# Decode step with sliding-window attention and a squared-ReLU MLP: the first wo projection computed ahead of the last K unit's transposes

## The chip, the core and the metric

The kernel runs on one core of one Trainium2 chip. The metric is the device time of one execution in microseconds (us). The core has a matrix engine (PE, with its weight loads listed apart as PEld), a vector engine (DVE), a scalar engine (ACT), GpSimd (POOL) and a sync engine (SP) that here does nothing but start DMA transfers, one after the other in program order. Engines wait for each other through semaphores; an instruction that waits holds up all that stand behind it on its own engine.

## The reference

One token for each of two batch rows is normalised; attention over the last 2048 positions of a cache, and an MLP, are computed from it and added to the input:

```python
B, Sq, D = x.shape                      # 2, 1, 576
Hq, Dh = 32, 128;  Hkv = 16             # two query heads per K/V head
W = min(4096, max(256, Sk // 4))        # 2048 of 8192
q = (x @ wq) split into heads
scores = q . k[:, :, Sk - W:] * Dh ** -0.5
o = softmax(scores) . v[:, :, Sk - W:]
A = o.reshape(B, Sq, Hq * Dh) @ wo      # wo: 4096 x 576
h = relu(x @ w1 + b1) ** 2              # F = 4608
Bm = h @ w2 + b2
return x + A(layernorm(x)) + Bm(layernorm(x))
```

Everything is bf16. K and V windows (16.8 MB each), wq, wo (4.7 MB each), w1 and w2 (5.3 MB each) are read once, 53.6 MB in all; the output is 2 x 576.

## The kernel before

**Units.** The work on the caches is cut into NU = 8 units. A unit u is four K/V heads of one batch row: a K tile and a V tile of 128 partitions x 8192 bf16 (2048 KB each). For each unit PE transposes K in eight groups of four (`transposes(u, g)`, tile kT_ps in PSUM), ACT and DVE copy the groups in turn into kT in SBUF, PE computes the scores (`scores`, sc_ps), DVE/POOL/ACT do the softmax (`softmax_max`, `softmax_exp`, `softmax_tr`, which leaves pT), PE multiplies by V (`pv`, pv_ps), DVE picks the wanted parts (`pv_mix`, tiles mix and acc) and PE sums them per head (`pv_out`, sm). `step(u, p, o)` is the pipeline: transposes and scores of unit u, softmax of u-1, the V product of p, the head sums of o.

**The wo projection.** wo is used in two halves of 2048 rows. When four units are done, `pv_out` lets DVE normalise them and write ws_t (t = 0 after unit 3, t = 1 after unit 7); `wo_acc(t)` is then 32 matmuls of 2 x 288 (16 rows of wo per partition, two column halves each), each with its own weight load of ws_t. They are accumulated into out_ps, the one PSUM tile that also collects the residual, b2 and most of the MLP's second product. The order of the sums within out_ps is free.

**The MLP.** w1 is used early (between units 1 and 2). The second product reads w2 in four parts: w2_0, w2_1, w2_2 (18 matmuls of 2 x 288 each into out_ps, `mlp_o`), and w2_3, loaded in two pieces of 7 and 2 rows (`mlp_tail`, into tail_ps). out_ps is copied to SBUF (part, line 555) and added into tail_ps by eight small matmuls; then tail_ps is copied out and stored.

**Buffers.** K, V and the first three w2 tiles take turns in one pool of six buffers (`kvpool`); w2_3 takes the buffer that held w1. The pool for wo, `wopool`, has **one** buffer: the transfer of the second half, wo_1, has to wait until the first half's last matmul has read wo_0.

**Order.** Each engine runs its instructions in a fixed order. PE's, and most of DVE's and ACT's, follow the program text (`keep_in_program_order`). SP's list of transfers is arranged when the program is built; it follows the text but for small shifts. All large loads go through SP and one DMA queue.

**The end of the program.** The lines that the change and the prediction's steps touch are the last 35 of the kernel: the transfers of the second wo half (line 534, issued at line 118) and of w2 (lines 535 and 536, issued at line 131), `step(NU - 1, NU - 3, NU - 4)`, that is, the transposes of unit 7 with the V product of unit 5 and the head sums of unit 4 (line 537), the V product of unit 6 (539, 540), `wo_acc(0)` (546), the V product of unit 7 (548) and, behind it, the first w2 part, `wo_acc(1)`, and the other w2 parts (550 to 560). Matmuls other than transposes are recorded at line 84, transposes at line 87, loads of K and V at line 106.

Of the kernel before, what the change touches and what calls it, by code (L numbers as in the profile page):

```python
# [16 lines left out]
def kernel(  # L17
# [105 lines left out]
    def issue_w2(g, r0, r1):  # L123
        if g < NG4 - 1:
            tl = kvpool.tile([P, FR * D], BF16, tag="kv", name=f"w2_{g}")[:]
        else:
            if r0 == 0:
                w2_last.append(wbig.tile([P, FR * D], BF16, tag="wbig", name=f"w2_{g}"))
            tl = w2_last[0][:, r0 * D:r1 * D]
        rows = B_w2[g * HW:(g + 1) * HW, :].rearrange("(p r) n -> p (r n)", r=FR)  # L130
        nc.sync.dma_start(out=tl, in_=rows[:, r0 * D:r1 * D])  # L131
        w2_tiles[(g, r0)] = tl
# [99 lines left out]
    def out_acc(lhsT, rhs_of, start=False, stop=False):  # L232
        for i in range(2):
            pe_mm(out_ps[32 * i:32 * i + B, :], lhsT=lhsT, rhs=rhs_of(i * OH, (i + 1) * OH),
                  start=start, stop=stop, skip_group_check=True)
# [36 lines left out]
    def transposes(u, g):  # L272
        k_sb = k_tiles[u]
        w, gw = divmod(g, GW)
        if gw == 0:
            kT_tiles[(u, w)] = ktpool.tile([P, NT, P, 2], BF16, tag="kT_sb", name=f"kT_{u}_{w}")
        kT = kT_tiles[(u, w)]
        kT_ps = psum.tile([P, PG, P], F32, tag="kT", bufs=3, name=f"kT_ps_{u}_{g}")
        for i in range(PG):
            q = g * PG + i  # L280
            pe_tr(out=kT_ps[:, i, :], in_=k_sb[:, 2 * q * Dh:2 * (q + 1) * Dh].bitcast(F32),
                                identity=ident_f[:])
        src = kT_ps[:].rearrange("p i s -> p (i s)").bitcast(BF16)
        dst = kT[:, gw * PG:(gw + 1) * PG, :, :].rearrange("p i s e -> p (i s e)")
        if g % 2 == 0:
            pin(nc.scalar.copy(out=dst, in_=src))  # L286
        else:
            pin(nc.vector.tensor_copy(out=dst, in_=src))  # L288

    def scores(u, w):  # L290
        tq, b = divmod(u, B)
        if w == 0:
            sc_tiles[u] = psum.tile([P, NT, 32], F32, tag="sc", bufs=2, name=f"sc_ps_{u}")
            pe_mm(sc_tiles[u][:].rearrange("p t s -> p (t s)"), lhsT=qhead[:], rhs=khead[:],
                             start=True, stop=False, skip_group_check=True)
        sc_ps = sc_tiles[u]
        kT = kT_tiles.pop((u, w))[:].rearrange("p t s e -> p e t s")
        for e in range(2):
            for k in range(4):
                pe_mm(sc_ps[32 * k:32 * (k + 1), :, :],  # L300
                                      lhsT=qz[:, e, b * NQ + tq, w, :, :].rearrange("p j c -> p (j c)"),
                                      rhs=kT[:, e, :, 32 * k:32 * (k + 1)], start=False, stop=(w == 1 and e == 1),
                                      skip_group_check=True, tile_position=(0, 32 * k))
# [3 lines left out]
    def softmax_max(u):  # L307
        sc_ps = sc_tiles.pop(u)[:].rearrange("p t s -> p (t s)")
        mx = work.tile([P, 1], F32, tag="mx", name=f"mx_{u}")
        pin(nc.vector.tensor_reduce(out=mx[:], in_=sc_ps, axis=AX.X, op=ALU.max))  # L310
        m2 = work.tile([P, NC], F32, tag="m2", name=f"m2_{u}")
        pin(nc.vector.tensor_scalar(out=m2[:], in0=offm[:], scalar1=mx[:, 0:1], scalar2=None, op0=ALU.add))  # L312
        gmax = work.tile([P, NC], F32, tag="gmax", name=f"gmax_{u}")
        nc.gpsimd.partition_all_reduce(gmax[:], m2[:], channels=P, reduce_op=ReduceOp.max)  # L314
        sm_cur[u] = (sc_ps, gmax)

    def softmax_exp(u):
        sc_ps, gmax = sm_cur.pop(u)
        gs = work.tile([P, NC], F32, tag="gs", name=f"gs_{u}")
        pin(nc.vector.tensor_tensor(out=gs[:], in0=gmax[:], in1=own_s[:], op=ALU.mult))  # L320
        nb = work.tile([P, 1], F32, tag="nb", name=f"nb_{u}")
        pin(nc.vector.tensor_reduce(out=nb[:], in_=gs[:], axis=AX.X, op=ALU.add))  # L322
        pr = work.tile([P, NT * 32], BF16, tag="pr", name=f"pr_{u}")
        acc = keep.tile([P, Dh + 1], F32, tag="acc", bufs=4, name=f"acc_{u}")
        pin(nc.scalar.activation(out=pr[:], in_=sc_ps, func=ACT.Exp, bias=nb[:], scale=scale, accum_out=acc[:, Dh:Dh + 1]))  # L325
        sm_cur[u] = (pr, acc)

    def softmax_tr(u):
        pr, acc = sm_cur.pop(u)
        pT = keep.tile([P, NT, 32], BF16, tag="pT", name=f"pT_{u}")  # L330
        pin(nc.vector.transpose(out=pT[:].rearrange("p t m -> p (t m)"), in_=pr[:]))  # L331
        pT_tiles[u], acc_tiles[u] = pT, acc
# [3 lines left out]
    def pv_start(u):  # L336
        pv_cur[u] = psum.tile([P, 4, Dh], F32, tag="misc", name=f"pv_ps_{u}")

    def pv(u, i):
        pv_ps = pv_cur[u]  # L340
        v = v_tiles[u][:].rearrange("p (w t x) -> p t w x", w=2, t=NT)
        for k in range(4):
            t = 4 * i + k
            pe_mm(pv_ps[32 * k:32 * (k + 1), :, :].rearrange("m (w a) d -> m w (a d)", w=2),
                                  lhsT=pT_tiles[u][:, t, :], rhs=v[:, t, :, :], start=(i == 0),
                                  stop=(i == NT // 4 - 1), skip_group_check=True, tile_position=(0, 32 * k))
# [21 lines left out]
    def pv_out(u):  # L368
        tq, b = divmod(u, B)
        t, half = divmod(tq, 2)  # L370
        if u % (2 * B) == 0:
            sm_tiles[t] = psum.tile([P, B, Dh + 1], F32, tag="sm", name=f"sm_{t}")
        sm = sm_tiles[t]
        pe_mm(sm[half * (P // 2):(half + 1) * (P // 2), b, :],
                         lhsT=tohead[:].rearrange("p c x -> p (c x)"), rhs=acc_tiles.pop(u)[:], start=True, stop=True,
                         skip_group_check=True, tile_position=(0, half * (P // 2)))
        if u % (2 * B) == 2 * B - 1:
            ri = work.tile([P, B], F32, tag="ri", name=f"ri_{t}")
            pin(nc.vector.reciprocal(out=ri[:], in_=sm[:, :, Dh]))
            od = work.tile([P, B, DW, WR], F32, tag="od", bufs=1, name=f"od_{t}")  # L380
            for k in range(B):
                nc.vector.scalar_tensor_tensor(out=od[:, k, :, :],
                                               in0=sm[:, k, 0:Dh].rearrange("p (x r) -> p x r", x=DW),
                                               scalar=ri[:, k:k + 1],
                                               in1=own[:].unsqueeze(2).to_broadcast([P, DW, WR]),
                                               op0=ALU.mult, op1=ALU.mult)
            ws = work.tile([P, WR, B], BF16, tag="ws", name=f"ws_{t}")
            with nc.allow_low_precision(reason="sums of one value and zeros"):
                nc.vector.tensor_reduce(out=ws[:], in_=od[:].rearrange("p b x r -> p r b x"), axis=AX.X, op=ALU.add)
            wo_state[t] = ws  # L390

    def wo_acc(tq):
        ws = wo_state.pop(tq)
        wo_sb = wo_tiles.pop(tq)
        for r in range(WR):
            out_acc(ws[:, r, :], lambda a, z: wo_sb[:, r, a:z])
# [86 lines left out]
    def step(u, p=None, o=None):  # L483
        if p is not None:
            pv_start(p)
        transposes(u, 0)
        softmax_max(u - 1)
        transposes(u, 1)
        softmax_exp(u - 1)
        transposes(u, 2)  # L490
        if p is not None:
            pv(p, 0)
        transposes(u, 3)
        if p is not None:
            pv(p, 1)
        softmax_tr(u - 1)
        if o is not None:
            pv_out(o)
        transposes(u, 4)
        scores(u, 0)  # L500
        for g in range(GW + 1, NG):
            transposes(u, g)
        for i in range(2, NR):
            if p is not None:
                pv(p, i)
        if p is not None:
            pv_mix(p)
        scores(u, 1)
# [25 lines left out]
    issue_wo(1)  # L534
    for w in W2P:
        issue_w2(*w)
    step(NU - 1, NU - 3, NU - 4)
    pv_start(NU - 2)
    for i in range(NR):
# [3 lines left out]
    softmax_exp(NU - 1)  # L543
    pv_mix(NU - 2)
    softmax_tr(NU - 1)
    wo_acc(0)
    pv_out(NU - 2)
    pv_all(NU - 1)
    pv_out(NU - 1)
# [48 lines left out]
```

## Time and profile before

| what | value |
|---|---|
| time, median of 3 runs (lowest to highest) | 139.25 us (138.78 to 139.61) |
| time of the profiled execution | 139.34 us |
| its span, first to last instruction | 137.6 us |
| mean granted PE clock | 0.876 |
| busy: PE, PEld | 88.7 us (64%), 54.9 us (40%) |
| busy: DVE, ACT, POOL | 59.6 us (43%), 43.9 us (32%), 7.7 us (6%) |
| read from HBM | 53.62 MB, 390 GB/s over the span |
| SP's DMA queue, share of 16 DMA engines | 92.2% |

How to read the profile: the page cuts the span into 40 equal slices of 3.44 us and gives for each how busy an engine was and what the DMA engines moved. The chain is followed back from the last instruction to whatever released each step. A timeline row gives start, duration, engine, line, operation, output tile and inputs, and in brackets how long the engine had been idle before and what ended the idle time. A windows row gives for a stretch of time its length, the busy time of PE, PEld, DVE, ACT and POOL (with the number of instructions), then the granted PE clock as a share of full speed, the busy share of the DMA engines and the rate in GB/s. "SPq" is the time that SP takes to issue a transfer, not the transfer.

### The profile page before, as it was taken

What the parts mean: (1) busy time and instruction counts of PE and PEld (TensorE: products, weight loads), DVE (VectorE), ACT (ScalarE), POOL (GpSimd) and SP (SyncE); (2) the same over time, 40 slices, a digit from 0 to 9 for tenths busy, and PEclk for the clock granted to TensorE, in tenths of its full rate; (3) what the DMA queues carried; (4) which work ended last, traced back from release to release, by engine and by line L of the source; (5) the groups of instructions that cost most, each with busy time, mean ns of one, the idle gap of its engine ahead of it and who ended that gap; (6) DMA issues with size and microseconds to landing.
All of it is one profiled execution on the core that took longest, in us unless ns stands there. A gap on an engine that the chain in (4) does not pass through costs nothing.

```text
span 137.6 us, 2040 instructions
## 1 busy us (share of the span) xinstructions
PE 88.7 (64%) x830; PEld 54.9 (40%) x830; DVE 59.6 (43%) x151; ACT 43.9 (32%) x63; POOL 7.7 (6%) x26
## 2 busy tenths in 40 slices
PE   0079047979967486696595797991059969408451
PEld 0078012919623454453451743650055524204230
DVE  6935202025551085458449247786005376700021
ACT  2627101014710467282272273670025402000001
POOL 7600000001000010100100100101000010000000
PEclk9999965555899999999999599999555999995999
DMA  4999979999989999999999999999999974799940
GB/s 153 408 514 397 493 326 448 419 426 543 422 346 424 410 453 419 424 453 405 434 453 400 443 441 410 444 426 420 443 434 419 427 302 80 316 401 431 426 194 1
DMA packets 3632, 53.74 MB, mean 391 GB/s; under 512 B 412, under 2 KB 420, under 8 KB 680
## 3 DMA queue, kind: packets, MB, share of 16 engines
q1 hardware_dynamic: 3604, 53.61, 92.2%
q8 instruction: 6, 0.10, 0.3%
q10 hardware_dynamic: 20, 0.01, 0.0%
q14 instruction: 2, 0.02, 0.0%
HBM read 53.62 MB, written 0.00 MB: 390 GB/s over the span
## 4 chain that ended last, share of the span: by engine, by line
DMA 66%; PE 24%; DVE 4%; ACT 2%; SPq 1%; issue 1%; DVEq 0%; ACTq 0%
DMA k<-in_A_k_cache_dram 41%; DMA wq_sb<-in_A_wq_dram 13%; DMA w<-in_B_w_dram 12%; PE kT_ps L87 10%; PE sc_ps L84 3%; PE q_ps L84 3%; PE qs_ps L84 3%; PE pv_ps L84 2%; DVE kT L288 2%; PE out_ps L84 2%; PE sm L84 1%; PE tail_ps L84 1%; ACT kT L286 1%; SPq L131 1%; ACT pr L325 1%
## 5 line engine op out<-in xcount | busy, mean ns | idle before, releaser
L87 PE MATMUL kT_ps<-ident_f,k 128*128 128x128 f32 x256 | 40.6, 314 | 14.4 <-DMA k<-in_A_k_cache_dram 14.0
L286 ACT COPY kT<-kT_ps 128x1024 bf16<-128x1024 bf16 x32 | 32.0, 1010 | 37.3 <-PE kT_ps L87 36.9
L87 PEld LDWEIGHTS kT_ps<-ident_f,k 128*128 128x128 f32 x256 | 33.5, 162 | 23.8 <-issue 20.2
L288 DVE COPY kT<-kT_ps 128x1024 bf16<-128x1024 bf16 x32 | 22.1, 691 | 32.7 <-PE kT_ps L87 32.6
L84 PE MATMUL sc_ps<-kT,qz 128*32 128x512 bf16 x128 | 10.6, 414 | 4.3 <-DVE kT L288 2.8
L84 PE MATMUL pv_ps<-v,pT 128*32 128x512 bf16 x128 | 10.8, 404 | 0.8 <-DVE acc L360 0.8
L314 POOL PARTITION_ALL_REDUCE gmax<-m x8 | 2.9, 365 | 103.9 <-DVE m L312 103.9
L84 PE MATMUL out_ps<-wo,ws 128*2 128x288 bf16 x64 | 5.7, 348 | 4.1 <-DMA wo<-in_A_wo_dram 4.1
L325 ACT ACTIVATE pr<-sc_ps,nb 128x512 bf16<-128x512 f32 x8 | 5.5, 687 | 8.4 <-DVE nb L322 8.4
L84 PE MATMUL q_ps<-wq_sb,xnT 128*4 128x512 bf16 x36 | 4.0, 628 | 5.2 <-DMA wq_sb<-in_A_wq_dram 5.2
L566 ACT CAST fin_sb<-tail_ps 2x144 bf16<-2x144 f32 x2 | 0.5, 272 | 20.3 <-PE tail_ps L84 20.2
L310 DVE TENSOR_REDUCE mx<-sc_ps 128x1 f32<-128x512 f32 x8 | 5.5, 684 | 3.1 <-PE sc_ps L84 3.1
L84 PEld LDWEIGHTS <-xnT 128*4 128x4 bf16 x90 | 2.6, 98 | 10.2 <-issue 9.3
L84 PEld LDWEIGHTS <-qz 128*32 128x32 bf16 x128 | 2.3, 98 | 9.9 <-DVE kT L288 6.2
L555 DVE COPY part<-out_ps 2x288 f32<-2x288 f32 x2 | 0.9, 448 | 12.0 <-PE out_ps L84 12.0
L360 DVE SCALAR_TENSOR_TENSOR mix<-pv_ps,own_j,mix 128x128 f32<-128x128 f32 x16 | 5.6, 351 | 0.6
L84 PEld LDWEIGHTS <-ws 128*2 128x2 bf16 x64 | 3.2, 100 | 6.4 <-issue 3.8
L331 DVE STREAM_TRANSPOSE pT<-pr 128x512 bf16<-128x512 bf16 x8 | 5.6, 702 | 0.2 <-ACT pr L325 0.2
L87 PE MATMUL pro_ps<-ident,xs 2*128 2x2 bf16 x10 | 0.6, 164 | 7.6 <-DVE xs L182 7.6
L84 PE MATMUL out_ps<-w,hT_sb 128*2 128x288 bf16 x54 | 3.8, 285 | 2.2 <-DMA w<-in_B_w_dram 2.2
L84 PEld LDWEIGHTS <-pT 128*32 128x32 bf16 x128 | 2.7, 95 | 5.4 <-issue 3.0
L84 PEld LDWEIGHTS <-hT_sb 128*2 128x2 bf16 x90 | 2.8, 83 | 5.2 <-issue 2.8
(77 smaller groups left out, 61.6 us busy)
## 6 DMA issues: line engine op xcount, KB each, us to landing
k<-in_A_k_cache_dram SPq DMA_DIRECT2D x8, 2048.0 KB, 7.4
v<-in_A_v_cache_dram SPq DMA_DIRECT2D x8, 2048.0 KB, 18.0
w_sb<-in_B_w_dram SPq DMA_DIRECT2D x1, 5184.0 KB, 19.1
wq_sb<-in_A_wq_dram SPq DMA_DIRECT2D x1, 4608.0 KB
wo<-in_A_wo_dram SPq DMA_DIRECT2D x2, 2304.0 KB, 8.7
w<-in_B_w_dram SPq DMA_DIRECT2D x3, 1296.0 KB
w<-in_B_w_dram SPq DMA_DIRECT2D x1, 1008.0 KB
w<-in_B_w_dram SPq DMA_DIRECT2D x1, 288.0 KB
```

Source lines behind the costliest of these rows:

```text
L84: return tc.keep_in_program_order(nc.tensor.matmul(out, **kw))
L87: return tc.keep_in_program_order(nc.tensor.transpose(**kw))
L131: nc.sync.dma_start(out=tl, in_=rows[:, r0 * D:r1 * D])
L286: pin(nc.scalar.copy(out=dst, in_=src))
L288: pin(nc.vector.tensor_copy(out=dst, in_=src))
L310: pin(nc.vector.tensor_reduce(out=mx[:], in_=sc_ps, axis=AX.X, op=ALU.max))
L314: nc.gpsimd.partition_all_reduce(gmax[:], m2[:], channels=P, reduce_op=ReduceOp.max)
L325: pin(nc.scalar.activation(out=pr[:], in_=sc_ps, func=ACT.Exp, bias=nb[:], scale=scale, accum_out=acc[:, Dh:Dh + 1]))
L331: pin(nc.vector.transpose(out=pT[:].rearrange("p t m -> p (t m)"), in_=pr[:]))
L360: op = nc.vector.scalar_tensor_tensor(out=nx, in0=pv_ps[:, j, :], scalar=own_j[:, j:j + 1], in1=acc, op0=ALU.mult, op1=ALU.add)
L555: nc.vector.tensor_copy(out=part[:, i * OH:(i + 1) * OH], in_=out_ps[32 * i:32 * i + B, :])
L566: cp(out=fin_sb[:, q * OQ:(q + 1) * OQ], in_=mlp["out"][32 * k:32 * k + B, :])
```

## The change

One call moves. `wo_acc(0)` stood between the softmax transposition of unit 7 and the head sums of unit 6; it now stands ahead of the last `step`.

```diff
     issue_wo(1)
     for w in W2P:
         issue_w2(*w)
+    wo_acc(0)
     step(NU - 1, NU - 3, NU - 4)
     pv_start(NU - 2)
     for i in range(NR):
...
     softmax_exp(NU - 1)
     pv_mix(NU - 2)
     softmax_tr(NU - 1)
-    wo_acc(0)
     pv_out(NU - 2)
     pv_all(NU - 1)
     pv_out(NU - 1)
```

On PE, before, the scores of unit 6 (sc_ps_999) are followed at once by the transposes of unit 7 (k_821 is its K tile, pT_982 the softmax of unit 5):

```order
 L84 MATMUL sc_ps_999<-kT_1_992,qz 32x512
-L87 MATMUL kT_ps_0_1063<-ident_f,k_821 128x128 x4
-L87 MATMUL kT_ps_1_1075<-ident_f,k_821 128x128 x4
-L87 MATMUL kT_ps_2_1088<-ident_f,k_821 128x128 x4
-L84 LDWEIGHTS pT_982
```

In the changed program the 32 weight loads and 32 matmuls of the first wo half (wo_819 is wo_0, ws_990 is ws_0) stand in between; the last of them and what follows:

```order
+L84 LDWEIGHTS ws_990
+L84 MATMUL out_ps<-wo_819,ws_990 2x288
+L87 MATMUL kT_ps_0_1095<-ident_f,k_821 128x128 x4
+L87 MATMUL kT_ps_1_1107<-ident_f,k_821 128x128 x4
+L87 MATMUL kT_ps_2_1120<-ident_f,k_821 128x128 x4
```

So 64 PE instructions go from behind the softmax of unit 7 to ahead of its transposes; nothing else on PE changes place.

On SP the end of the list of transfers changes as well. Names: v_931 and v_933 are the V tiles of units 6 and 7, wo_1050 is wo_1, w_0 to w_3 the parts of w2; in brackets stand the semaphores that a transfer waits for before it is issued (DMAHW: an earlier transfer has landed; PE: PE has come far enough):

```order
 L106 DMA v_931<-in_A_v_cache_dram 128x1x8192 [waits DMAHW0_49,PE_49]
 L106 DMA v_933<-in_A_v_cache_dram 128x1x8192 [waits DMAHW7_49,PE_49]
-L131 DMA w_0_1052<-in_B_w_dram 128x5184 [waits DMAHW2_49,PE_49]
-L118 DMA wo_1050<-in_A_wo_dram 128x9216 [waits DMAHW4_49,DMAHW1_49,PE_49]
+L118 DMA wo_1050<-in_A_wo_dram 128x9216 [waits DMAHW4_49,PE_49]
+L131 DMA w_0_1052<-in_B_w_dram 128x5184 [waits DMAHW2_49,DMAHW1_49]
 L131 DMA w_1_1054<-in_B_w_dram 128x5184
-L131 DMA w_2_1056<-in_B_w_dram 128x5184 [waits DMAHW5_49,DMAHW3_49]
+L131 DMA w_2_1056<-in_B_w_dram 128x5184 [waits DMAHW5_49,DMAHW3_49,PE_49]
 L131 DMA w_3_1058<-in_B_w_dram 128x4032
 L131 DMA w_3_1058<-in_B_w_dram 128x1152
```

wo_1 changes places with w2_0 and is now the first transfer behind the last V tile, and w2_2 has a wait for PE of its own. The instructions of DVE, ACT and POOL keep their order.

## The prediction

> **What bounds the kernel now.** I read the page first: its span, the rate of the DMA engines slice by slice, and the shares of the chain that ended last.
>
> ```profile
> span 137.6 us, 2040 instructions
> GB/s 153 408 514 397 493 326 448 419 426 543 422 346 424 410 453 419 424 453 405 434 453 400 443 441 410 444 426 420 443 434 419 427 302 80 316 401 431 426 194 1
> DMA 66%; PE 24%; DVE 4%; ACT 2%; SPq 1%; issue 1%; DVEq 0%; ACTq 0%
> ```
>
> The transfers run at 400 to 450 GB/s nearly everywhere, and two thirds of the chain is DMA: this is a stream of bytes with arithmetic beside it. The exception is late: slices 32 to 34 of the 40 (110 to 120 us) show 302, 80 and 316 GB/s. Next the chain in order of time, from the landing of the last K tile on, says what the stream waited for there.
>
> ```profile
> 74.18 26.99 DMA k<-in_A_k_cache_dram
> ...
> 113.38 2.07 PE out_ps L84 x32
> 115.47 0.33 SPq L118
> ...
> 116.81 16.70 DMA w<-in_B_w_dram
> 133.55 1.29 PE tail_ps L84 x44
> ```
>
> PE's 32 matmuls of the first wo half end at 115.45, SP issues wo_1 at 115.47, the last large transfer lands at 133.51 (116.81 + 16.70), PE's last 44 matmuls end at 134.84. SP's own waits after 86 us, and its timeline, give the reason.
>
> ```profile
> SPq L118 <- PE out_ps L84: 19.1, 1, 19.1
> SPq L131 <- PE kT_ps L87: 6.2, 1, 6.2
> SPq L118 <- DMA wo<-in_A_wo_dram: 3.9, 1, 3.9
> ```
> ```profile
> 83.89 1.18 SPq L106 DMA_DIRECT2D v<-in_A_v_cache_dram  x2
> 92.14 0.33 SPq L131 DMA_DIRECT2D w<-in_B_w_dram  x1
> 115.86 2.19 SPq L131 DMA_DIRECT2D w<-in_B_w_dram  x4
> ```
>
> SP issued V of units 6 and 7 at 84 and w2_0 at 92.14, and then stood at wo_1 from 92.47 to 115.47: 3.9 us for the landing of wo_0 (at 96.4) and 19.1 for wo_acc(0) to free the only wo buffer. The remaining w2 transfers stood behind it. What was queued did not last that long:
>
> ```profile
> 86.07:101.17 15.10, 7.20 (x67) 4.25 (x67) 7.78 (x19) 4.67 (x6) 0.73 (x2) 0.85 1.00 429
> 101.17:112.00 10.83, 9.65 (x71) 5.84 (x75) 5.01 (x12) 4.71 (x6) 0.00 (x0) 0.74 1.00 426
> 112.00:119.00 7.00, 5.29 (x72) 2.62 (x74) 4.41 (x13) 0.78 (x2) 0.36 (x1) 1.00 0.47 146
> ```
>
> From 112 to 119 only 7.00 x 146 = 1022 GB/s x us = 1.02 MB moved, which at 426 takes 2.40 us. **The hole in the stream is 7.00 - 2.40 = 4.60 us**, with the slow restart in it.
>
> **The change part by part.** It adds no instruction and no byte. It moves 32 matmuls with their weight loads, and through the wo buffer the issue of wo_1. PE's timeline shows where they come from and go to.
>
> ```profile
> 86.07 1.50 PE L87 MATMUL kT_ps<-ident_f,k 128*128 128x128 f32 x12 [0.81 <-DMA k<-in_A_k_cache_dram]
> ...
> 92.89 0.62 PE L84 MATMUL sc_ps<-kT,qz 128*32 128x512 bf16 x8 [0.24 <-DVE kT L288]
> 101.30 2.79 PE L87 MATMUL kT_ps<-ident_f,k 128*128 128x128 f32 x12 [7.80 <-DMA k<-in_A_k_cache_dram]
> ...
> 110.55 0.62 PE L84 MATMUL sc_ps<-kT,qz 128*32 128x512 bf16 x8 [0.24 <-DVE kT L288]
> ...
> 113.31 2.12 PE L84 MATMUL out_ps<-wo,ws 128*2 128x288 bf16 x32
> ...
> 115.81 1.05 PE L84 MATMUL pv_ps<-v,pT 128*32 128x512 bf16 x16
> 118.56 0.41 PE L84 MATMUL sm<-acc,tohead 128*64 128x129 f32 x2 [1.71 <-DVE acc L360]
> 118.90 1.27 PE L84 MATMUL out_ps<-w,hT_sb 128*2 128x288 bf16 x18
> 124.22 3.60 PE L84 MATMUL out_ps<-wo,ws 128*2 128x288 bf16 x32 [4.06 <-DMA wo<-in_A_wo_dram]
> ...
> 131.12 1.27 PE L84 MATMUL out_ps<-w,hT_sb 128*2 128x288 bf16 x18 [2.20 <-DMA w<-in_B_w_dram]
> ```
> ```profile
> 90.58 0.58 DVE L389 TENSOR_REDUCE ws<-od 128x32 bf16<-128x256 f32 x1
> 115.05 0.70 DVE L331 STREAM_TRANSPOSE pT<-pr 128x512 bf16<-128x512 bf16 x1
> 119.85 0.58 DVE L389 TENSOR_REDUCE ws<-od 128x32 bf16<-128x256 f32 x1
> 132.42 0.93 DVE L555 COPY part<-out_ps 2x288 f32<-2x288 f32 x2 [11.99 <-PE out_ps L84]
> ```
>
> *Where it goes.* PE is idle from 93.51 to 101.30, waiting for K of unit 7, which landed at 101.17. ws_0 is ready at 91.16 and wo_0 at 96.4, so the 32 matmuls start at 96.4. They took 2.12 us at full clock and 3.60 us mostly at half clock; behind an idle PE I take 3.60. They end at 100.0, 1.2 us ahead of K: **cost nothing, hidden by the wait for K**. If wo_0 came later than about 97.6, each us would push the transposes back by one.
>
> *Where it goes away.* Unit 7's V product at 115.81 starts on its softmax (115.05 + 0.70 = 115.75), not on wo_acc(0). Taking the 2.12 us out from ahead of it gives at most 0.06 us there: I count nothing.
>
> *The transfers.* wo_1 is issued at 100.0 instead of 115.47, w2_0 and w2_1 right behind it. w2_0 loses its place at 92.14, but the two V tiles in front keep the engines busy until about 111, so nothing is lost. w2_2 now waits by itself for PE; if that is the buffer of unit 7's K tile, its last transpose is done by 111.2 even at the pace of before, when wo_1, w2_0 and w2_1 are still to move. The stream then never runs dry: **-4.60 us**. What was in the hole was nothing but the wait, and what is late next is the stream itself.
>
> As a check I add up the landings from the sizes on the page.
>
> ```profile
> v<-in_A_v_cache_dram SPq DMA_DIRECT2D x8, 2048.0 KB, 18.0
> wo<-in_A_wo_dram SPq DMA_DIRECT2D x2, 2304.0 KB, 8.7
> w<-in_B_w_dram SPq DMA_DIRECT2D x3, 1296.0 KB
> w<-in_B_w_dram SPq DMA_DIRECT2D x1, 1008.0 KB
> w<-in_B_w_dram SPq DMA_DIRECT2D x1, 288.0 KB
> ```
>
> At the 429 GB/s of the stretch before K's landing, 2048 KB take 4.89 us, 2304 take 5.50, 1296 take 3.09, 1008 take 2.41 and 288 take 0.69. From 101.17 on: V at 106.1 and 111.0, wo_1 at 116.5, w2_0 at 119.5, w2_1 at 122.6, w2_2 at 125.7, the pieces of w2_3 at 128.1 and 128.8. The same sum with the hole gives 133.4 for before, against 133.51 on the chain. So the gain lies between 4.60 and 133.51 - 128.8 = 4.7; I take 4.60, the measured hole, and the last landing at 128.9.
>
> [...]
>
> *Is PE ready by then?* Unit 7's step, from its first transpose to its last score, took 9.87 us (101.30 to 111.17); unit 6's, at full clock, 7.44 (86.07 to 93.51). With wo_acc(0) run just ahead, the clock may be up again. So ws_1, ready at 120.43 before, comes between 118.0 and 120.4. w2_0 lands at 119.5: its 18 matmuls end at 120.9, wo_acc(1) at 123.0 to 124.5, w2_1's at 125.8 at the latest, and w2_2's start on the landing at 125.7 and end at 127.1. The copy to part (0.93) ends at 128.0, ahead of 128.9. From the last landing on, all is as before: 133.51 to the end of the span. **PE's tail costs 0, at most 0.5 us** if it runs at half clock at first.
>
> *Sum.* The profiled execution took 139.34 us (span 137.6, and 1.74 around it), the median was 139.25, 0.09 less. 139.34 - 4.60 = 134.74; beside the median 134.65. I predict **134.7 us**.
>
> **The rivals.**
>
> *The buffer isn't freed early.* The wait of wo_1 for PE could stand for a later instruction, such as the end of unit 7's step. Then wo_1 is issued at 111.2. The V tiles end 3.1 us before the stream stopped (112.0 + 0.58 us for the bytes moved up to 114, less the 3.1 of w2_0, which is now behind): at 109.5. The hole would be 1.7 us plus what the restart cost (4.60 less 115.47 - 112.58 = 2.89, so 1.7): 3.4 instead of 4.6, **138.1 us**; held as long as before, no change. For it speaks only that a semaphore count is not seen in the trace; against it, that SP in the old run was released at 115.47, at the last of the 32 matmuls (115.45), while other PE work went on. 5 in 100, 2 of them no change.
>
> *PE at half clock becomes the bound.*
>
> ```profile
> 96.00:98.00 2.00, 0.00 (x0) 0.00 (x0) 0.00 (x0) 0.00 (x0) 0.00 (x0) 0.64 0.94 401
> 124.00:126.00 2.00, 1.78 (x16) 0.99 (x17) 0.00 (x0) 0.00 (x0) 0.00 (x0) 0.50 1.01 430
> 126.00:128.00 2.00, 2.00 (x26) 1.17 (x22) 0.00 (x0) 0.00 (x0) 0.00 (x0) 0.68 0.99 418
> ```
>
> The granted clock fell from 1.00 to 0.50 at 96.6 (0.64 of the stretch), 3 us after PE stopped at 93.51, and came back at 127.3 (0.68), 3 us after it set in at 124.22. In the changed kernel PE idles from about 116 to 119.5 and may start w2_0 at half clock. In the 3.06 us at half clock the old wo_acc(1) did some 24 of 32 matmuls, 0.13 us each. If the clock stayed down to the end: w2_0 119.5 to 121.8, wo_acc(1) to 126.0, w2_1 to 128.3, w2_2 to 130.7, and the 44 small matmuls (1.29 doubled) to 133.3, against 134.84 before: **137.8 us**. It decides only if the clock doesn't come back within about 6 us of work, and at 127.3 it came back after 3.1; 4 in 100. [...]
>
> *The early transfers slow down V: slower than before.* Were the queue shared rather than served in turn, wo_1, w2_0 and w2_1, issued at 100, would take bandwidth from the V tiles. Five shares of 426 GB/s: the w2 parts (1.33 MB) end after 15.6 us, V (0.77 MB left in each) after about 5.4 more, at 122.2. Units 6 and 7 then need 2.75 each (115.81 to 118.56), and 1.87 go to ws_1 (118.56 to 120.43): 129.6. wo_acc(1) 2.12, two w2 parts 2.54, part 0.93, the last 16 of the 44 small matmuls 0.5: 135.7 on PE, 0.8 later than before: **140.1 us**. It decides once V lands later than about 121.4. Against it: K of unit 7 landed 15.1 us after K of unit 6 (101.17 less 86.07), and V, wo_0 and K between (6.55 MB) at 429 GB/s take 15.3, so the V tiles issued at 84 and w2_0 took nothing from it. 3 in 100.
>
> **How the numbers follow.** The forecast has 88 in 100, the late buffer 5, the half clock 4, slower by sharing 3. The forecast's own bounds are a gain of 4.7 and no cost at PE (134.6) to 4.6 with 0.5 at PE (135.2), with the 0.6 below and 0.4 above by which the runs of before spread around the median: 134.0 to 135.7. That holds nearly all of the 88, so no rival need be reached; I round outward to 133.9 and 135.9. About 0.5% is what a measurement here tells from no change: faster by more 95 (88 + 3 + 4), within it 2, slower 3.
>
> **What would show it.** Right: 32 out_ps matmuls on wo in PE's old idle stretch at about 96.4 to 100; wo_1 issued at about 100 and not 115; no slice under 380 GB/s from 110 to 125; the last w2 landing near 128.9; K of unit 7 still at 101.2. A step is wrong if SP still stands at wo_1 after 102, if the transposes of unit 7 start after 101.5, if V lands after 112, or if PE, not a landing, releases the last matmuls. The whole is wrong if the rate in the old hole rises and falls elsewhere by as much.

## The result and the profile after

| | before | after |
|---|---|---|
| median (lowest to highest) | 139.09 us (138.78 to 139.61), 4 runs | 134.22 us (134.19 to 134.33), 4 runs |
| profiled execution, its span | 139.34 us, 137.6 us | 134.33 us, 132.5 us |
| ratio, 95% interval | | 0.9647 (0.9616 to 0.9679) |

The change takes 4.87 us off the median and 5.01 us off the profiled execution; 4.60 were forecast. (Ratios here and below leave out runs more than 1.5% above the fastest of the same kernel, which matters where a kernel has ten runs.)

The page of the changed kernel, the same three lines as before the change:

```profile
span 132.5 us, 2040 instructions
GB/s 105 443 445 501 389 381 430 430 483 513 401 403 359 430 410 455 411 460 401 465 396 445 425 415 453 415 456 432 423 410 445 415 440 433 414 432 423 418 216 1
DMA 71%; PE 21%; DVE 2%; ACT 2%; issue 1%; SPq 1%; DVEq 0%; ACTq 0%
```

The dip is gone: from 96 us on no slice is under 410 GB/s until the stream ends in the last but one. SP's timeline and its waits behind 84 us say why:

```profile
84.23 2.06 SPq L106 DMA_DIRECT2D v<-in_A_v_cache_dram  x2
99.93 0.33 SPq L118 DMA_DIRECT2D wo<-in_A_wo_dram  x1
100.36 11.17 SPq L131 DMA_DIRECT2D w<-in_B_w_dram  x5
```
```profile
SPq L118 <- DMA wo<-in_A_wo_dram: 10.2, 1, 10.2
SPq L131 <- PE kT_ps L87: 8.8, 1, 8.8
...
SPq L118 <- PE out_ps L84: 3.4, 1, 3.4
```

wo_1 is issued at 99.93 instead of 115.47. SP comes to it earlier than before, with w2_0 no longer ahead of it, and stands there 10.2 us for the landing of wo_0; but then it waits only 3.4 us for wo_acc(0), where it had waited 19.1. w2_2 has a wait of 8.8 us for unit 7's transposes, with V, wo_1 and two w2 parts still to be moved meanwhile. The windows show both stretches of the old dip:

```profile
101.17:112.00 10.83, 9.87 (x67) 6.05 (x67) 4.58 (x10) 4.72 (x6) 0.00 (x0) 0.71 1.01 432
112.00:119.00 7.00, 2.90 (x37) 1.08 (x37) 4.84 (x14) 0.78 (x2) 0.37 (x1) 0.91 0.99 423
```

423 GB/s between 112 and 119, where there had been 146. PE's timeline:

```profile
93.11 0.62 PE L84 MATMUL sc_ps<-kT,qz 128*32 128x512 bf16 x8 [0.24 <-DVE kT L288]
96.56 3.35 PE L84 MATMUL out_ps<-wo,ws 128*2 128x288 bf16 x32 [2.82 <-DMA wo<-in_A_wo_dram]
101.50 2.79 PE L87 MATMUL kT_ps<-ident_f,k 128*128 128x128 f32 x12 [1.60 <-DMA k<-in_A_k_cache_dram]
...
110.99 0.62 PE L84 MATMUL sc_ps<-kT,qz 128*32 128x512 bf16 x8 [0.24 <-DVE kT L288]
...
119.84 2.32 PE L84 MATMUL out_ps<-w,hT_sb 128*2 128x288 bf16 x18 [0.18 <-DMA w<-in_B_w_dram]
121.95 3.42 PE L84 MATMUL out_ps<-wo,ws 128*2 128x288 bf16 x32
125.20 2.37 PE L84 MATMUL out_ps<-w,hT_sb 128*2 128x288 bf16 x36
128.48 0.61 PE L84 MATMUL tail_ps<-w,hT_sb 128*2 128x144 bf16 x28 [0.90 <-DMA w<-in_B_w_dram]
```

The 32 matmuls stand in the old idle stretch and end at 99.91; K of unit 7 still lands at about 101.4 (101.17 before). At the end PE waits 0.90 us for the last landing at 128.43, which came at 133.51 before: 5.08 us earlier, and the span is 5.1 shorter. The whole gain is in that landing.

### The profile page after: what moved, and what is told of

Same layout as the page of the kernel before. It is cut to its first block, busy times and chain, and to the rows that moved or that the text cites. A ratio compares the mean times of both kernels' runs of the same rounds, so it can differ in the third digit from the quotient of the medians.

```text
span 132.5 us, 2040 instructions
## 1 busy us (share of the span) xinstructions
PE 91.7 (69%) x830; PEld 56.6 (43%) x830; DVE 59.7 (45%) x151; ACT 43.9 (33%) x63; POOL 7.7 (6%) x26
## 4 chain that ended last, share of the span: by engine, by line
DMA 71%; PE 21%; DVE 2%; ACT 2%; issue 1%; SPq 1%; DVEq 0%; ACTq 0%
DMA k<-in_A_k_cache_dram 44%; DMA w<-in_B_w_dram 13%; DMA wq_sb<-in_A_wq_dram 13%; PE kT_ps L87 10%; PE sc_ps L84 4%; PE q_ps L84 3%; PE qs_ps L84 1%; PE pv_ps L84 1%; DVE kT L288 1%; PE tail_ps L84 1%; PE sm L84 1%; ACT kT L286 1%; ACT pr L325 1%; DVE qrow L252 1%; SPq L106 0%
## 5 line engine op out<-in xcount | busy, mean ns | idle before, releaser
L87 PE MATMUL kT_ps<-ident_f,k 128*128 128x128 f32 x256 | 41.7, 322 | 6.3 <-DMA k<-in_A_k_cache_dram 6.2
L87 PEld LDWEIGHTS kT_ps<-ident_f,k 128*128 128x128 f32 x256 | 35.2, 168 | 15.2 <-issue 12.0
L84 PE MATMUL out_ps<-wo,ws 128*2 128x288 bf16 x64 | 6.8, 391 | 2.8 <-DMA wo<-in_A_wo_dram 2.8
L84 PEld LDWEIGHTS <-xnT 128*4 128x4 bf16 x90 | 3.1, 116 | 12.9 <-issue 12.7
L84 PE MATMUL h_ps<-w_sb,xnT 128*4 128x384 bf16 x54 | 4.3, 483 | 3.7 <-DMA w_sb<-in_B_w_dram 3.7
L84 PE MATMUL sm<-acc,tohead 128*64 128x129 f32 x16 | 4.0, 334 | 3.5 <-DVE acc L360 3.5
L84 PEld LDWEIGHTS <-ws 128*2 128x2 bf16 x64 | 3.7, 112 | 5.8 <-issue 3.1
L433 DVE TENSOR_TENSOR hs<-hT_ps,hodd 128x20 f32<-128x20 f32 (+1 forms) x4 | 0.5, 173 | 10.3 <-ACT hodd L430 10.3
```

Source lines behind the costliest of these rows:

```text
L84: return tc.keep_in_program_order(nc.tensor.matmul(out, **kw))
L87: return tc.keep_in_program_order(nc.tensor.transpose(**kw))
L433: nc.vector.tensor_tensor(out=hs[:].rearrange("p (g r) b -> p r g b", g=NG4)[:, r0:r0 + n, g:g + 2, :], in0=even[:, :, g:g + 2, :], in1=od ...
```

## The experiments

Two theories were set against each other. **Buffer theory:** the gain is the hole in the transfers, and the hole was SP's wait for the only wo buffer. **PE theory:** the gain comes from 32 matmuls leaving PE's last stretch. The change does both at once.

**Memory of its own for wo_1.** PE's order is as before; wo_1 is put beside w2_3 into the room that w1 leaves.

```diff
-        tl = wopool.tile([P, WR, D], BF16, tag="wo_sb", name=f"wo_{t}")
+        if t == 0:
+            tl = wopool.tile([P, WR, D], BF16, tag="wo_sb", name=f"wo_{t}")
+        else:
+            big = wbig.tile([P, (FR + WR) * D], BF16, tag="wbig", name="w2_wo")
+            w2_last.append(big)
+            tl = big[:, FR * D:].rearrange("p (r n) -> p r n", r=WR)
...
-            if r0 == 0:
-                w2_last.append(wbig.tile([P, FR * D], BF16, tag="wbig", name=f"w2_{g}"))
```

> The kernel before, with wo_acc(0) at its old place, but wo_1 has memory of its own (the room that w1 leaves, beside w2_3). Buffer theory (the gain is the hole in the transfers, and the hole is the wait for wo_0's buffer): wo_1 is issued near 85 us, the rate from 112 to 119 is above 400 GB/s, 134.2 us. PE theory (the gain is that 32 matmuls leave PE's tail): as before, 139.1 us.

Measured: 134.32 us (134.11 to 135.01), ratio 0.9675 (0.9615 to 0.9735). Its SP and PE rows and its window (line 118 has become line 123 by the edit):

```profile
85.43 0.88 SPq L123 DMA_DIRECT2D w_wo<-in_A_wo_dram  x1
```
```profile
113.61 2.12 PE L84 MATMUL out_ps<-wo,ws 128*2 128x288 bf16 x32
```
```profile
112.00:119.00 7.00, 5.02 (x70) 2.54 (x70) 4.70 (x14) 0.78 (x2) 0.37 (x1) 1.00 1.00 427
```

The 32 matmuls are where they always were, at 113.61, and the gain is there in full. This refutes the PE theory.

**Last row late.** The changed kernel, but one of the 16 rows of wo_0 is left for the old place (`wo_acc` takes a range of rows for it).

```diff
-    wo_acc(0)
+    wo_acc(0, 0, WR - 1)
     step(NU - 1, NU - 3, NU - 4)
...
     softmax_tr(NU - 1)
+    wo_acc(0, WR - 1, WR)
     pv_out(NU - 2)
```

> The changed kernel, but the last 2 of the 32 matmuls of wo_acc(0) stay at the old place, so that the wo buffer is freed late although PE's work has moved. Buffer theory: wo_1 is issued near 113.9, and w2_0, which now stands behind it, as well; the queue runs dry at 109.5, the hole is 4.4 plus 1.7 for the restart, 134.3 + 6.1 = 140.4 us, slower than before. PE theory: 134.2 us.

Measured: 138.32 us in the profiled execution, median 139.79 of ten runs (138.09 to 140.93), ratio 0.9996 (0.9944 to 1.0049) from six of the ten. 30 of the 32 matmuls have moved, and the gain is gone.

```profile
101.44 1.50 PE L87 MATMUL kT_ps<-ident_f,k 128*128 128x128 f32 x12 [1.24 <-DMA k<-in_A_k_cache_dram]
...
111.02 0.29 PE L84 MATMUL out_ps<-wo,ws 128*2 128x288 bf16 x2
```
```profile
111.34 0.33 SPq L118 DMA_DIRECT2D wo<-in_A_wo_dram  x1
```
```profile
108.00:110.00 2.00, 0.96 (x20) 0.34 (x20) 1.89 (x6) 0.09 (x1) 0.00 (x0) 1.00 0.69 295
```

SP issues wo_1 right behind the last two matmuls, at 111.34, and the stream is already running out between 108 and 110: w2_0, which stood ahead of wo_1 before the change, is now behind it. I had reckoned with 113.9 and 140.4. In this execution PE ran unit 7's step at full clock (1.00 granted from 101.17 to 112.00; the first twelve transposes took 1.50 us instead of 2.79), so that the issue came 2.56 earlier, which makes 137.8 of the 140.4, against 138.32. The executions without a trace lie up to 2.6 us higher; that they are those with the half clock is an inference, and the mean granted clock bears it out only in part: it is lowest in the four slowest (0.825 to 0.838), but highest in the three at 139.8 (0.855 to 0.864 against 0.841 to 0.854 in the three fastest).

**Behind the step.** The kernel before, wo_acc(0) moved by a shorter way, ahead of unit 6's V product: a smaller dose of the same thing.

```diff
     step(NU - 1, NU - 3, NU - 4)
+    wo_acc(0)
     pv_start(NU - 2)
...
-    wo_acc(0)
     pv_out(NU - 2)
```

> The kernel before with all of wo_acc(0) directly behind unit 7's step, ahead of the V product of unit 6. Buffer theory: wo_1 is issued near 113.3 instead of 115.5; w2_0 stays ahead of it; the hole is 2.4 us instead of 4.6, 136.9 us. PE theory: nothing leaves PE's tail, and the V product of unit 6 comes later: 139.1 us or more.

Measured: 137.58 us (137.38 to 137.66), ratio 0.9895 (0.985 to 0.994): a gain, but 1.5 instead of 2.2 us.

```profile
113.24 0.33 SPq L118 DMA_DIRECT2D wo<-in_A_wo_dram  x1
```
```profile
131.06 1.01 PE L84 MATMUL tail_ps<-w,hT_sb 128*2 128x144 bf16 x28 [1.17 <-DMA w<-in_B_w_dram]
132.00 0.66 PE L84 MATMUL tail_ps<-part,ident_f 2*2 2x144 f32 x8
132.59 0.41 PE L84 MATMUL tail_ps<-w,hT_sb 128*2 128x144 bf16 x8
```

wo_1 was issued at 113.24, as reckoned, and the last landing came 2.5 us earlier than in the kernel before (131.0 against 133.5). The missing part is behind it: the last 44 matmuls ran at half clock (0.60 granted from 130 to 132, 0.50 from 132 to 133.5) and took 1.94 us (131.06 to 133.00) instead of the 1.2 of the changed kernel (128.48 to 129.66), 0.8 more.

**w2_0 first again.** In the changed kernel w2_0 is issued ahead of wo_1, as it had been.

```diff
-    issue_wo(1)
-    for w in W2P:
+    issue_w2(*W2P[0])
+    issue_wo(1)
+    for w in W2P[1:]:
         issue_w2(*w)
```

> The changed kernel with w2_0 issued ahead of wo_1 again, as before the change. Both theories: the two V tiles in front hide which comes first, 134.2 us. If the place of w2_0 matters by itself, the time differs by more than 0.5 us.

Measured: 134.20 us (134.14 to 134.96), ratio 0.9667 (0.9617 to 0.9717). The swap on SP that came with the change counts nothing.

**wo_1 last.** All w2 transfers go ahead of wo_1, and PE does wo_acc(1) behind the w2 parts. Nothing is freed earlier; the wait just holds nobody up. (The flag that ends the sum in out_ps moves along.)

```diff
-    issue_wo(1)
     for w in W2P:
         issue_w2(*w)
+    issue_wo(1)
...
-    mlp_o(*W2P[0])
-    wo_acc(1)
-    for w in W2P[1:NG4 - 1]:
+    for w in W2P[:NG4 - 1]:
         mlp_o(*w)
+    wo_acc(1)
```

> The kernel before, wo_acc(0) at its old place, with one buffer for wo, but SP issues all w2 transfers ahead of wo_1, and PE does wo_acc(1) behind the three w2 parts. Buffer theory: the w2 transfers no longer stand behind the wait, the stream has no hole (above 400 GB/s from 112 to 119) and ends near 128.8 with wo_1; behind that stand wo_acc(1) with 2.1 (full clock) to 3.6 us, the copy 0.9 and 16 small matmuls 0.65 instead of 44 with 1.3: 136.6 to 138.1 us. PE theory: nothing leaves PE's tail, 139.1 us or more.

Measured: 139.37 us (138.78 to 139.81, ten runs), ratio 0.9996 (0.9963 to 1.0028): no gain. The hole is closed and the expected time still missed.

```profile
112.00:119.00 7.00, 5.29 (x70) 2.70 (x64) 4.41 (x15) 0.78 (x2) 0.36 (x1) 0.95 1.01 431
```
```profile
129.18 3.19 PE L84 MATMUL out_ps<-wo,ws 128*2 128x288 bf16 x28 [5.85 <-DMA wo<-in_A_wo_dram]
...
133.15 0.89 PE L84 MATMUL tail_ps<-part,ident_f 2*2 2x144 f32 x8
133.97 0.29 PE L84 MATMUL tail_ps<-w,hT_sb 128*2 128x144 bf16 x8
```

431 GB/s in the old dip, and the last landing at 129.1: the stream is as short as in the changed kernel to within 0.7 us. But it is now wo_1 that lands last, and behind it stand 32 matmuls, mostly at half clock (129.18 to 132.62; 0.53 granted from 130 to 132), the copy to part and 16 small matmuls: PE ends at 134.3, against 134.7 before. The profiled execution took 138.89, 0.8 over my upper bound; of that 0.3 is the later landing and about 0.4 a slip in my sum (128.8 + 3.6 + 0.9 + 0.65 is 133.95, 0.8 ahead of the 134.74 at which PE ends in the kernel before, which makes 138.5 and not 138.1). The median of the ten lies another 0.5 higher, which no trace explains. A closed hole is worth what stands behind the last landing lets through.

**Early matmuls twice, and six times.** The changed kernel with the call repeated ahead of the step; what it adds to out_ps more than once is part of its output.

```diff
+    wo_acc(0)
     wo_acc(0)
     step(NU - 1, NU - 3, NU - 4)
```

> The changed kernel with the 32 early matmuls done twice, so that they outlast the wait for K (the first wo half counts double in the output). It tells how much slack stands behind unit 7's K. The 64 matmuls end at 102 to 104 instead of 99.9. If unit 7's step then runs at half clock as before, PE is 2.3 us late at wo_acc(1) and the end comes at 135.4; if the clock is up by then, 134.2. Were unit 7's step on the path that sets the end, 136.5 to 138 us.

> The changed kernel with the 32 early matmuls done six times (the first wo half counts six times in the output), to see from where PE becomes the bound. At full clock 192 matmuls take 12.5 us from 96.6 and end at 109; unit 7's transposes start 7.5 us late. The stream is not touched (w2_2 is issued near 115, when about 7 us of transfers are still queued). ws_1 is ready near 125.5; with wo_acc(1) 2.1, two w2 parts 2.4, part 0.9 and 16 small matmuls 0.7 PE ends at 131.6 instead of 129.7: 136.2 us; 138 or more at half clock. If the early matmuls cost what they take, as they would without slack behind unit 7's K, it is 134.3 + 7.5 = 141.8.

Measured: twice, 134.26 us (134.18 to 134.33), ratio 0.9636 (0.9591 to 0.9681); six times, median 140.04 of ten runs (137.62 to 140.6), ratio 0.9953 (0.9905 to 1.0001) from the five of 137.62 to 139.6. PE with the call twice, and then PE and SP with it six times:

```profile
96.61 4.08 PE L84 MATMUL out_ps<-wo,ws 128*2 128x288 bf16 x64 [1.16 <-DMA wo<-in_A_wo_dram]
101.54 1.50 PE L87 MATMUL kT_ps<-ident_f,k 128*128 128x128 f32 x12 [0.85 <-DMA k<-in_A_k_cache_dram]
...
108.36 0.61 PE L84 MATMUL sc_ps<-kT,qz 128*32 128x512 bf16 x8 [0.24 <-DVE kT L288]
```
```profile
96.69 13.60 PE L84 MATMUL out_ps<-wo,ws 128*2 128x288 bf16 x192 [2.85 <-DMA wo<-in_A_wo_dram]
110.22 1.53 PE L87 MATMUL kT_ps<-ident_f,k 128*128 128x128 f32 x12
```
```profile
110.32 0.33 SPq L118 DMA_DIRECT2D wo<-in_A_wo_dram  x1
```

The doubled call did not do what it was made for: PE was idle for only 1.16 us ahead of it, the granted clock was 1.00 from 96 to 102, 64 matmuls took 4.08 us and ended at 100.7, still ahead of K. But it shows something else. Unit 7's step ended at 108.97 instead of 111.61 in the changed kernel, 2.6 us earlier, and the time is the same to 0.04 us: PE's pace in that step is not on the path. Six times, PE does become the bound, in the profiled execution at least. This is one of the five slowest (140.51 us; the others took 137.6 to 139.6 and left no trace). In it the step starts 8.7 us late and PE's last matmul ends at 135.9 instead of 129.7, 6.2 late. wo_1 waits for all 192 as well, which opens a new hole that my 136.2 left out (issue at 110.32, 279 GB/s from 108 to 110), but that was not the limit here: behind the 192, PE waits for no transfer. What I had too small is PE's own work, partly at half clock (0.50 granted from 98 to 100 and from 122 to 130): the 192 end 1.3 us later than my 109, and wo_acc(1) took 3.42 instead of 2.1. How much of this holds for the faster executions, 1.4 to 3.4 above the 136.2, is open; none was as slow as the 141.8 without slack.

**Both ways at once.** Early call and memory of its own.

> Both ways to free the stream at once: wo_acc(0) early as in the changed kernel, and memory of its own for wo_1. Buffer theory: there is no hole left to close, 134.2 us. If any part of the gain were PE's, it would come on top of the 134.3 us of the kernel with memory of its own and the old order: 133.7 us or less.

Measured: 134.24 us (134.17 to 134.46), ratio 0.9636 (0.9598 to 0.9674). Nothing is added.

**The last loads as 4 and 5 rows.** The one attempt at a faster kernel.

```diff
-    W2P = [(0, 0, 9), (1, 0, 9), (2, 0, 9), (3, 0, 7), (3, 7, 9)]
+    W2P = [(0, 0, 9), (1, 0, 9), (2, 0, 9), (3, 0, 4), (3, 4, 9)]
```

> The changed kernel with w2_3 loaded as 4 and 5 rows instead of 7 and 2, to see whether the 44 matmuls behind the last landing can be shortened. If the first piece lands by itself early enough, 16 of its matmuls and the eight of part are done before the last landing, and 20 remain: 133.7 to 133.9 us. If both pieces land together, as in the changed kernel: 134.2 us.

Measured: 134.16 us (134.13 to 134.4), ratio 0.9631 (0.9593 to 0.9669): no difference from the changed kernel that can be told.

```profile
127.30 0.42 PE L84 MATMUL tail_ps<-w,hT_sb 128*2 128x144 bf16 x16
127.72 0.89 PE L84 MATMUL tail_ps<-part,ident_f 2*2 2x144 f32 x8
129.01 0.48 PE L84 MATMUL tail_ps<-w,hT_sb 128*2 128x144 bf16 x20 [0.41 <-DMA w<-in_B_w_dram]
```

24 of the 44 matmuls did get out of the way, but the second piece landed at 128.97, 0.54 later than the landing that released the 44 in the changed kernel. No kernel tried is faster than the changed one by more than the noise.

**The kernel before, twice more.** One execution each.

> The kernel before once more, to see whether its spread of 138.2 to 140.3 us is the moment at which wo_1 is issued. If so: where unit 7's step runs at full clock longer than in the first trace, wo_1 is issued before 115.5 and the time is shorter than 139.34 by as much; where it runs at half clock longer, both are later by as much.

> As before_again_1: time less the moment of wo_1's issue stays at 139.34 - 115.47 = 23.9 us within 0.4.

The issue of wo_1 in the first and in the second:

```profile
115.36 0.33 SPq L118 DMA_DIRECT2D wo<-in_A_wo_dram  x1
```
```profile
115.12 0.33 SPq L118 DMA_DIRECT2D wo<-in_A_wo_dram  x1
```

They took 139.10 and 139.06 us. Time less issue: 23.74 and 23.94, against 23.87 in the first trace. The distance stays within 0.2 us, as expected, but three issues within 0.35 us are too close together to explain a spread of 2 us.

## Why the prediction was right

- **The hole.** Forecast: 4.60 us, by rate. Measured: the last landing moved by 5.08. The mechanism is right, the term is 0.5 too small. My count stopped at 119, taking the restarted stream for a whole one; it ran at 417 GB/s from 119 to 132, while the changed kernel's ran at 432 and 423 in its two stretches above. 13 us at 1.4 to 3.5% less would make 0.2 to 0.5. But unbroken streams vary as much: with both ways at once the same two stretches read 437 and 415. That a restarted stream is slower is therefore not shown, and where the 0.5 comes from stays open.
- **The early matmuls cost nothing.** Forecast: 96.4 to 100.0. Measured: 96.56 to 99.91, and K's transposes follow K's landing. They start at 101.50, the very bound that I had set for a wrong step, but because K landed 0.19 later than before; PE had then been idle for 1.60 us.
- **The old place gives nothing.** With memory of its own for wo_1 the old place costs nothing either; with 30 of 32 matmuls gone from it, nothing is gained.
- **The transfers.** Forecast: issue at 100.0, last landing at 128.9. Measured: 99.93 and 128.43. The swap with w2_0 counts nothing behind two V tiles, as forecast. Where the issue is late, as in the last-row kernel, it should cost w2_0's 3.1 us of transfers in the queue; that is reckoned, no run there has w2_0 in front.
- **PE's tail.** The cost was 0, as taken, but the margin was thinner than I had it. I let the clock come up before unit 7's step; it did not (0.50 granted from 98 to 106), and the step took 10.11 us (101.50 to 111.61), outside my 7.44 to 9.87. ws_1 was ready at 121.13 instead of 118.0 to 120.4, wo_acc(1) ended near 125.4 instead of 123.0 to 124.5, and the copy to part, forecast to end at 128.0, ended only with the last landing:

```profile
127.61 0.93 DVE L555 COPY part<-out_ps 2x288 f32<-2x288 f32 x2 [6.49 <-PE out_ps L84]
```

  It is done at 128.54; the matmuls that need it start at 129.02, behind the 28 that need only w2_3. So 0.5 us of room was left.
- **The rivals.** The buffer was freed by the last of the 32 matmuls, not later: SP issued wo_1 0.02 us behind it. V was not slowed down to where it would count: the V product of unit 6 (at 112.41) waits for DVE and that of unit 7 (at 116.24) for its softmax, neither for a landing. The half clock came, from about 117.8 on (0.50 granted from 118 to 124), and went at about 124.6, 4.8 us after PE set in at 119.84 and before it cost anything; that it can cost was seen behind the step (0.8 us) and with wo_1 last (32 matmuls in 3.44 us, against 2.12 at full clock).

## What to carry to other kernels

Where a stream of transfers bounds a kernel, look for the one dip in its rate and ask what the issuing engine waited for there; a tile with one buffer holds up not only its own next load but all loads queued behind it (19.1 us for wo_1 here, with four w2 transfers behind it), and the last reader of the old tile sets the time, even if it is 2 matmuls of 32 (an issue at 111.34 instead of 99.93). Move that reader into an idle stretch, or give the load memory of its own; they gave 4.9 and 4.7 us here. And see what lands last: closing the same hole with the wrong transfer at the end gave nothing.

## What the runs showed of the hardware

The same 2.82 us of idle PE ahead of the early matmuls, with the same work on PE up to there, was followed by half clock in one execution and not in another. In the changed kernel the clock fell at 97.3, while PE was already at work again, and 32 matmuls took 3.35 us; with both ways at once it stayed up, they took 2.12, and it fell at 101.6 (1.00 granted from 100 to 101, 0.59 from 101.5 to 102), behind a second idle stretch (2.79 us). The first row is the window of the changed kernel, the other two are the window and the PE row of the kernel with both ways:

```profile
98.00:100.00 2.00, 1.90 (x16) 0.82 (x12) 0.00 (x0) 0.00 (x0) 0.00 (x0) 0.50 0.94 401
```
```profile
98.00:100.00 2.00, 0.72 (x12) 0.30 (x8) 0.00 (x0) 0.00 (x0) 0.00 (x0) 1.00 1.01 434
```
```profile
96.60 2.12 PE L84 MATMUL out_ps<-wo,ws 128*2 128x288 bf16 x32 [2.82 <-DMA wo<-in_A_wo_dram]
```

When the clock changed can be worked out from the rows, if it is taken to be either 1.00 or 0.50, as in 16 of the 20 stretches of 2 us from 90 to 130 of the changed kernel: a mean of 0.82 over 2 us is 0.72 us at half clock. These are the four changes of the changed kernel from 90 to 130, down, up, down and up:

```profile
96.00:98.00 2.00, 1.44 (x18) 0.93 (x19) 0.00 (x0) 0.00 (x0) 0.00 (x0) 0.82 1.01 434
106.00:108.00 2.00, 2.00 (x11) 1.04 (x7) 1.23 (x2) 0.25 (x2) 0.00 (x0) 0.62 1.01 426
116.00:118.00 2.00, 1.10 (x17) 0.33 (x16) 0.81 (x3) 0.00 (x0) 0.00 (x0) 0.94 1.01 430
124.00:126.00 2.00, 2.00 (x32) 1.26 (x29) 0.00 (x0) 0.00 (x0) 0.00 (x0) 0.85 1.04 428
```

They come out at 97.28, 107.52, 117.76 and 124.60. In the kernel before, a fall comes out at 96.56 and a return at 127.28 (0.64 and 0.68 in the prediction's rows). The falls do not stand at one distance from the idle time ahead of them: the one at 96.56 came 3.05 us after PE had stopped; the one at 97.28 came 0.72 us after PE had set in again behind 2.82 us of idle time; and the one at 117.76 came 0.47 us after a V product of 1.05 us. What sets these moments the runs do not show.

```profile
116.24 1.05 PE L84 MATMUL pv_ps<-v,pT 128*32 128x512 bf16 x16 [0.18 <-DVE pT L331]
```

The times of the kernels in which transfers wait long for PE also spread more: ten runs of the last-row kernel over 2.8 us and each set of thirteen runs of the kernel before over 1.5 to 1.7, against 0.1 to 0.9 in the sets of four of the kernels at 134 us. The sets differ in size, and that the clock is the cause is not shown.
